# Two sink operations, smaller projection groups in batch 0, and more work that GpSimd and VectorE share, in a planned attention and mixture kernel

## The chip, the cores and the metric

One core of a Trainium2 chip runs the whole kernel in one launch. The metric is device time in microseconds, from several runs. The profile is of one more execution, taken by the hardware profiler.

## What is computed

The input x of a second attention is the output of a first one.

```python
# first: q, k, v of (4, 8, 768, 64); n_sink = 4, window = 128
scores = q @ k^T / 8
keep = (column < 4) | (0 <= row - column < 128)
x = softmax(where(keep, scores, -1e9)) @ v            # -> (4, 768, 512)
# second: four experts e, each with a causal attention over 768 rows, 64 wide
logits = x @ w_gate                                    # (.., 4); the two largest, softmax of both
y_e = softmax(causal(x wq[e] (x wk[e])^T / 8)) @ (x wv[e]) @ wo[e]
out = sum over the two chosen e of weight_e * y_e
```

Float32 is wanted at nearly full precision. The kernel splits an operand into a high part (float32r) and a low part (the rest) and adds three products: high by high, high by low, low by high.

## The kernel before, in words

**Tiling.** The 768 rows of a batch are six row blocks of 128. The first attention is worked in units of one batch and one pair of heads (16 units, names such as "010": batch 0, pair 1, kind 0), the second in units of one batch and one pair of experts (8 units, "001" to "311", kind 1). In a banded unit row blocks 0 and 1 are one piece (edge_rows), blocks 2 and 3 and blocks 4 and 5 are a pair each (both_rows). A pair goes through: scores on TensorE (line 1398), a copy under a mask (1728) and a subtraction with a row minimum (1736) on VectorE, the exponential with its sum on ScalarE (1740), the sum of the parts (1440, 1442) and its inverse (1445), the normalisation by the inverse on GpSimd (1758), transposes on TensorE (1457) which ScalarE or VectorE copy out of PSUM (1254, 1256), a triangular mask on GpSimd (1514), and value products on TensorE (1424, 1428). For the part of a row's band that two blocks share, the kernel uses differences of neighbouring value blocks, dv, made by two GpSimd subtractions per unit (1645).

**Sinks.** A pair's tile p is 128 x 4 x 132: 128 band columns and 4 sink columns for each of four (row block, head). The sinks' weights go into a small tile, psk: two copies of the high part and one of the low part. The function keep makes them with three GpSimd operations (1749, 1753, 1754) from the weights before normalisation and the inverse, and the normalisation then takes the 512 band columns alone (1758). Sink values are multiplied with a selection into the tile vs, once a unit (spread, 1636).

**Weights.** The weights wv, wq, wk, wo are loaded, ScalarE makes the high parts (1189) and GpSimd the low parts (1193), 16 pieces of up to 260 columns.

**Second attention.** For a unit, q and k are projected with the matmuls of line 1831, in two groups of columns for all batches: row blocks 0 to 3 (512 columns) and 4 and 5 (256). A group waits for x of its row blocks from all four head pairs. ScalarE writes the high part (1313), VectorE the low part (1316). Values and gate logits come from line 1858, the output from line 1905.

**Order.** Nothing is issued in the order of the text. Each operation is a step with a priority, a cost for each engine that may run it, and the steps it waits for. Plan.emit simulates the engines and writes out one fixed order for each queue. It takes an engine's next step by readiness, and on TensorE by priority with a price for changing the kind of matmul (STAY, BULK) and one for waiting (HURRY). Table NUDGE adds a number to priorities, by name of step; table ONLY pins a step to one engine; ISSUE, MOVE_TIME and LANDING price transfers. Where TensorE would wait over 220 ns in the first 130 us of the plan, emit puts filler matmuls on the zero tile "nought" (1061, 1064). Transfers are issued by SP and ScalarE alone.

Of the kernel before, what the change touches and what calls it, by code (L numbers as in the profile page):

```python
# [10 lines left out]
F32 = mybir.dt.float32  # L11
# [23 lines left out]
for other in ("ROWS", "FULL", "cols", "rows"):  # L35
# [5 lines left out]
ISSUE, MOVE_TIME, LANDING = 1.4, 1.25, 400  # L41
# [23 lines left out]
    "differences_POOL": 77.0, "000 differences_POOL": -73.3, "000 differences_POOL 0": -19.3, "both_PE": 0.8,  # L65
# [760 lines left out]
    "311 fn_DVEACT 21": ACT, "311 store_SPACT 5": SP,  # L826
}

HURRY = 86.86
STAY = 50.53  # L830
BULK = -58.78
FILL_COST, FILL_KEEP, FILL_END = 220.0, 0.0, 130000.0
# [181 lines left out]
def kernel(  # L1014
# [14 lines left out]
    nc = tc.nc  # L1029
# [683 lines left out]
    def both_rows(prio, acc, i, pair, value, diff, vs, made_vs):  # L1713
# [43 lines left out]
        def norm():  # L1757
            nc.gpsimd.tensor_mul(p.t[:, :, :128], p.t[:, :, :128], f()[:, :, None].to_broadcast([128, 4, 128]))  # L1758
# [255 lines left out]
```

## Time and profile before

| what | value |
|---|---|
| time, median of 3 runs | 369.12 us (368.68 to 370.0) |
| the profiled execution, device time | 368.14 us |
| its span, first to last instruction | 366.2 us |
| TensorE matmul busy | 357.6 us, 98% |
| VectorE, ScalarE, GpSimd busy | 288.4, 262.3, 206.3 us |
| granted TensorE clock | 1.000 |

Matmuls overlap in the pipeline, so their busy time includes waiting that is hidden in it, and filler counts as busy. Where a row gives "x32 | 33.0, 1041", these are the count, the time in us in which at least one of them ran, and the mean ns of one; what follows a second bar is the engine's idle time before them.

### The profile page before, as it was taken

Reading aid. Unit: us, or ns where it says so; the run is one execution under the profiler, and the core shown is the slowest. Engines: PE = TensorE matmul, PEld = TensorE weight load, DVE = VectorE, ACT = ScalarE, POOL = GpSimd, SP = SyncE. Lnnn points to the kernel's source line nnn. Section 1 sums busy time; section 2 is a strip of 40 time slices with the busy share of each in tenths; the row PEclk is TensorE's granted clock in tenths of the full one; section 3 lists DMA queues with packets and bytes.
Section 4 is the critical chain, followed back from the end, with each engine's and each line's share of the span. In section 5 each row is a group of like instructions: output and inputs, shape, how many; then the busy total and the mean of one; then the engine's idle time right before and its main releaser. Section 6 shows DMA issues by size and latency. Waiting matters only on the chain.

```text
span 366.2 us, 13040 instructions
## 1 busy us (share of the span) xinstructions
PE 357.6 (98%) x4708; PEld 311.1 (85%) x4708; DVE 288.4 (79%) x1271; ACT 262.3 (72%) x928; POOL 206.3 (56%) x490
## 2 busy tenths in 40 slices
PE   8998999999999999999999999999999999999996
PEld 7767789988889889888888888988889889988884
DVE  4798979779989996369999988659799967476831
ACT  2778997459987996149888968536989957056951
POOL 5289999858558718326856973143658720160700
PEclk9999999999999999999999999999999999999999
DMA  9983988961281218322897898018920463049512
GB/s 178 177 199 70 184 148 165 170 114 46 47 152 24 48 25 156 95 89 69 243 252 116 199 248 165 2 57 318 238 39 3 135 220 80 2 174 294 140 59 115
DMA packets 134832, 48.10 MB, mean 131 GB/s; under 512 B 121776, under 2 KB 129456, under 8 KB 134768
## 3 DMA queue, kind: packets, MB, share of 16 engines
q1 hardware_dynamic: 108000, 38.75, 45.9%
q10 hardware_dynamic: 26768, 8.52, 9.7%
q8 instruction: 37, 0.61, 0.7%
q14 instruction: 27, 0.22, 0.2%
HBM read 30.88 MB, written 16.12 MB: 128 GB/s over the span
## 4 chain that ended last, share of the span: by engine, by line
PE 87%; DVE 6%; ACT 3%; DMA 2%; issue 1%; SPq 0%; ACTq 0%; DVEq 0%
PE b L1424 21%; PE b L1831 19%; PE b L1385 10%; PE b L1858 10%; PE b L1905 9%; PE b L1457 8%; PE b L1398 5%; PE b L1380 3%; PE b L1428 1%; DVE b L1728 1%; ACT p L1740 1%; DVE p L1736 1%; DVE p L1674 1%; DMA kn<-in_k_dram 1%; DMA qn<-in_q_dram 1%
## 5 line engine op out<-in xcount | busy, mean ns | idle before, releaser
L1610 ACT ACTIVATE p<-p,st 128x256 f32<-128x256 f32 (+5 forms) x96 | 63.5, 665 | 10.1 <-DVE st L1602 9.7
L1740 ACT ACTIVATE p<-p,st 128x132 f32<-128x132 f32 x128 | 51.0, 405 | 5.5 <-DVE st L1736 4.9
L1602 DVE CUSTOM_DVE_ANT_0 p<-b,cmask 128x384 f32<-128x384 f32 (+3 forms) x96 | 45.4, 502 | 2.0 <-ACT p L1263 1.4
L1385 PE MATMUL b<-ks,qs 64*128 64x384 f32 (+3 forms) x384 | 43.6, 341 | 0.0
L1254 ACT ACTIVATE pt<-b 128x256 f32<-128x256 f32 (+3 forms) x100 | 38.4, 416 | 3.2 <-PE b L1457 3.1
L1424 PE MATMUL b<-pt,vn 128*64 128x128 f32 x448 | 39.6, 281 | 0.3
L1457 PE MATMUL b<-ident,p 64*128 64x64 f32 x820 | 38.5, 227 | 0.3 <-POOL p L1758 0.3
L1440 POOL TENSOR_TENSOR st<-st 128x2 f32<-128x2 f32 (+1 forms) x50 | 9.8, 197 | 50.7 <-ACT p L1610 30.9
L1858 PE MATMUL b<-wvh,x 128*128 128x260 f32 x192 | 38.0, 284 | 0.0
L1457 PEld LDWEIGHTS b<-ident,p 64*128 64x128 f32 x820 | 32.4, 138 | 6.1 <-issue 2.2
L1256 DVE COPY pt<-b 128x256 f32<-128x256 f32 (+3 forms) x74 | 33.3, 464 | 4.8 <-PE b L1457 2.7
L1385 PEld LDWEIGHTS b<-ks,qs 64*128 64x128 f32 x384 | 31.1, 187 | 2.9 <-issue 0.7
L1905 PE MATMUL b<-woh,y 128*128 128x512 f32 x96 | 33.2, 400 | 0.0
L1758 POOL TENSOR_TENSOR p<-p,st 128x512 f32<-128x512 f32 x32 | 33.0, 1041 | 0.0
L1679 ACT ACTIVATE p<-p,st 128x128 f32<-128x128 f32 (+1 forms) x64 | 28.9, 454 | 5.5 <-DVE st L1674 5.3
L1831 PE MATMUL b<-x,wqh 128*128 128x512 f32 (+1 forms) x128 | 32.8, 341 | 0.0
L1831 PE MATMUL b<-x,wkh 128*128 128x256 f32 (+1 forms) x128 | 32.6, 341 | 0.0
L1736 DVE CUSTOM_DVE_ANT_0 p<-b,pair_mask 128x132 f32<-128x132 f32 x128 | 32.4, 285 | 0.0
L1858 PEld LDWEIGHTS b<-wvh,x 128*128 128x128 f32 x192 | 30.8, 188 | 0.9 <-DVE st L1445 0.2
L1424 PEld LDWEIGHTS b<-pt,vn 128*64 128x64 f32 x448 | 25.1, 136 | 4.7 <-issue 1.7
L1514 POOL TENSOR_SCALAR_AFFINE_SELECT pt<-pt 128x512 f32<-128x512 f32 x32 | 20.3, 635 | 13.4 <-ACT pt L1254 8.9
L1398 PE MATMUL b<-kx,qn 64*64 64x128 f32 (+2 forms) x768 | 26.1, 277 | 1.5 <-POOL kx L1328 1.5
(133 smaller groups left out, 1001.8 us busy)
## 6 DMA issues: line engine op xcount, KB each, us to landing
qn<-in_q_dram SPq DMA_DIRECT2D x46, 96.0 KB, 2.6
vn<-in_v_dram SPq DMA_DIRECT2D x22, 192.0 KB, 3.5
out_dram<-o ACTq DMA_DIRECT2D x15, 256.0 KB, 2.3
there<-u SPq DMA_DIRECT2D x5, 768.0 KB, 3.5
u<-there SPq DMA_DIRECT2D x20, 192.0 KB, 4.0
kn<-in_k_dram SPq DMA_DIRECT2D x38, 96.0 KB, 2.7
there<-u SPq DMA_DIRECT2D x5, 640.0 KB, 2.9
u<-there SPq DMA_DIRECT2D x20, 160.0 KB, 4.5
```

The source lines that it names most:

```text
L1254: nc.scalar.activation(dst(), src(), AF.Copy)
L1385: nc.tensor.matmul(o, self.qs.t[hs, a, qs], keys(hs, b), start=n == 0, stop=n == 2)
L1398: nc.tensor.matmul(o, self.q_of()[hs, q0 + 64 * h:q0 + 64 * h + 64], ks, start=True, stop=True)
L1424: nc.tensor.matmul(o[e * 64:e * 64 + 64], lhs, rhs, start=e not in self.begun, stop=last and self.done == len(self.steps))
L1457: nc.tensor.transpose(t[g].t[:, n, :], x[gs], ident[gs, gs])
L1602: nc.vector.tensor_tensor_reduce(out=one(e)[:, cs], in0=s2[e].t[:, :(c1 - c0) * 128], in1=mask(c0, c1), scale=times, scalar=st.t[:, 3, es] ...
L1610: nc.scalar.activation(x, x, AF.Exp, bias=st.t[:, 0, es], scale=-1.0, accum_out=st.t[:, 1, es])
L1736: nc.vector.tensor_tensor_reduce(out=p.t[:, n, :], in0=s2[e].t[:, 248 * r:248 * r + SW], in1=pair_mask, scale=-scale, scalar=BIG, op0=OP.a ...
L1740: nc.scalar.activation(p.t[:, n, :], p.t[:, n, :], AF.Exp, bias=st.t[:, 0, n:n + 1], scale=-1.0, accum_out=st.t[:, 1, n:n + 1])
L1831: nc.tensor.matmul(t.t, w[a][:, c, es], X[b, c].t[:, x, cs], start=c == 0 and m == 0, stop=c == NCH - 1 and m == 2)
L1858: nc.tensor.matmul(t.t[:, :VW], X[b, c].t[:, a, qs], W["wv"][w][:, c, :], start=c == 0 and n == 0, stop=c == NCH - 1 and n == 2)
L1905: nc.tensor.matmul(t.t, Y[b, c].t[:, a, qs], W["wo"][w][:, c, :], start=c == 0 and n == 0, stop=c == EP - 1 and n == 2)
```

## The change

Six edits in the kernel's text:

- Sinks. The normalisation takes all 528 columns of p and may run on GpSimd (one operation) or on ScalarE (four). After it a GpSimd copy writes the two high parts of the sinks, and a GpSimd subtraction the low part. The three operations of keep are gone.
- Projections of batch 0. Its column groups become row blocks 0 and 1, 2 and 3, 4 and 5. Batches 1 to 3 keep theirs.
- Low parts of the weights, the low part of the sinks' values, the spreads and the differences may run on VectorE as well as on GpSimd (by_either).
- The tables. NUDGE has some 3,050 entries before and after; of 2,822 names found in both, ten keep their number. ONLY grows from 402 to 442 pins. Among the new ones low parts 1, 10 and 12 are pinned to VectorE and eight to GpSimd, the spreads of units 020 and 100 to VectorE and nine to GpSimd, the differences of 110, 130, 210, 200, 220, 300 and 310 to VectorE and six to GpSimd (010, 020 and 030 among them). Of the pairs' normalisations 000 norm 3, 020 norm 2, 110 norm 2, 120 norm 3 and 330 norm 2 are pinned to ScalarE, nine to GpSimd. What isn't pinned the planner chooses.
- Planner's weights: HURRY 86.86 to 58.27, STAY 50.53 to 53.9, BULK -58.78 to -24.95.
- Transfer prices: ISSUE 1.4 to 1.3, MOVE_TIME 1.25 to 1.15, LANDING 400 to 250.

```diff
+    def by_either(prio, cost, fn, *rest, **more):
+        def go():
+            fn(nc.vector if s.eng == DVE else nc.gpsimd)
+        go.__qualname__ = fn.__qualname__
+        s = plan.step(prio, cost, go, *rest, **more)
+        return s
...
-                    prio + 3, {POOL: 700},
+                    prio + 3, {POOL: 700, DVE: 520},
...
-        lo = plan.step(SINK_VALUES + 1, {POOL: 2430}, lambda: nc.gpsimd.tensor_sub(
+        lo = by_either(SINK_VALUES + 1, {POOL: 2430, DVE: 1600}, lambda engine: engine.tensor_sub(
...
-            made_vs = plan.step(prio_of(max(first, 2)), {POOL: pool_cost(256)}, spread, SINKS[1], [vs], fifo="vs")
+            made_vs = by_either(prio_of(max(first, 2)), {POOL: pool_cost(256), DVE: 420}, spread, SINKS[1], [vs], fifo="vs")
...
-            differ = plan.step(..., {POOL: 2 * (260 + 1.7 * 64 * (end - d0))}, differences, ...)
+            differ = by_either(..., {POOL: 2 * (260 + 1.7 * 64 * (end - d0)), DVE: 1000}, differences, ...)
...
+        def norm():
+            if nm.eng == ACT:
+                for n in range(4):
+                    nc.scalar.activation(p.t[:, n, :], p.t[:, n, :], AF.Copy, scale=st.t[:, 2, n:n + 1])
+            else:
+                nc.gpsimd.tensor_mul(p.t, p.t, f()[:, :, None].to_broadcast([128, 4, SW]))
+        nm = plan.step(prio - LEAD_N, {POOL: pool_cost(4 * SW), ACT: 4 * (187 + 0.833 * SW)}, norm, [r], (), [p, st])
+
         def keep():
-            nc.gpsimd.tensor_mul(psk.t[:, :32]..., p.t[:, None, :, 128:SW]..., f()...)
-            low = psk.t[:, 32:48].rearrange("p (n s) -> p n s", s=4)
-            nc.gpsimd.tensor_mul(low, p.t[:, :, 128:SW], f()[:, :, None].to_broadcast([128, 4, 4]))
-            nc.gpsimd.tensor_sub(psk.t[:, 32:48], psk.t[:, 32:48], psk.t[:, :16])
-        kept = plan.step(prio - LEAD_N, {POOL: 672}, keep, [r], [psk], [p, st], fifo="psk")
-
-        def norm():
-            nc.gpsimd.tensor_mul(p.t[:, :, :128], p.t[:, :, :128], f()[:, :, None].to_broadcast([128, 4, 128]))
-        nm = plan.step(prio - LEAD_N, {POOL: pool_cost(512)}, norm, [r, kept], (), [p, st])
+            sinks = p.t[:, :, 128:SW]
+            nc.gpsimd.tensor_copy(psk.t[:, :32]..., sinks[:, None].to_broadcast([128, 2, 4, 4]))
+            nc.gpsimd.tensor_sub(psk.t[:, 32:48]..., sinks, psk.t[:, :16]...)
+        kept = plan.step(prio - LEAD_N, {POOL: 440}, keep, [nm], [psk], [p], fifo="psk")
...
-            second(b, n, cuts, rows, row, ...)
+            second(b, n, cut("0 2 4 6") if b == 0 else cuts, rows, row, ...)
```

## Rows read from the trace of the kernel before

**Rows 1.** The page's busy times: us, share of the span, instructions of each engine.

```profile
PE 357.6 (98%) x4708; PEld 311.1 (85%) x4708; DVE 288.4 (79%) x1271; ACT 262.3 (72%) x928; POOL 206.3 (56%) x490
```

**Rows 2.** Busy time by stretches of 10 us: the stretch and its length, then busy us and instructions of PE, PEld, DVE, ACT and POOL, the granted clock, the DMA share and GB/s.

```profile
10.00:20.00 10.00, 9.85 (x206) 7.94 (x206) 8.44 (x48) 7.39 (x34) 4.09 (x12) 1.00 1.02 180
20.00:30.00 10.00, 9.17 (x176) 6.97 (x170) 9.72 (x55) 8.38 (x37) 8.66 (x22) 1.00 0.80 170
30.00:40.00 10.00, 8.38 (x168) 7.09 (x166) 8.47 (x54) 8.93 (x39) 9.54 (x16) 1.00 0.53 100
40.00:50.00 10.00, 9.79 (x180) 7.80 (x177) 9.76 (x52) 10.00 (x44) 9.76 (x23) 1.00 0.85 170
50.00:60.00 10.00, 9.66 (x138) 8.61 (x138) 7.53 (x30) 7.54 (x29) 9.92 (x19) 1.00 0.80 155
...
80.00:90.00 10.00, 10.00 (x154) 8.73 (x152) 10.00 (x45) 9.79 (x34) 6.78 (x15) 1.00 0.18 42
...
140.00:150.00 10.00, 10.00 (x69) 9.20 (x68) 3.35 (x19) 3.90 (x16) 8.95 (x22) 1.00 0.82 158
...
270.00:280.00 10.00, 10.00 (x190) 8.90 (x191) 10.00 (x53) 10.00 (x44) 8.39 (x20) 1.00 0.01 3
```

**Rows 3.** The same table for the filler of line 1064 alone: PE and PEld busy us, with their instructions.

```profile
10.00:20.00 10.00, 3.89 (x52) 2.73 (x52) 1.00 1.02 180
20.00:30.00 10.00, 3.13 (x42) 2.17 (x44) 1.00 0.80 170
30.00:40.00 10.00, 1.90 (x36) 1.66 (x32) 1.00 0.53 100
40.00:50.00 10.00, 0.88 (x12) 0.64 (x12) 1.00 0.85 170
50.00:60.00 10.00, 0.00 (x0) 0.00 (x0) 1.00 0.80 155
```

**Rows 4.** The chain that ended last, share of the span by engine, from the page.

```profile
PE 87%; DVE 6%; ACT 3%; DMA 2%; issue 1%; SPq 0%; ACTq 0%; DVEq 0%
```

**Rows 5.** Pieces of that chain in order of time: start us, length us, what.

```profile
4.68 4.11 DMA kn<-in_k_dram
...
12.85 0.42 DVE b L1728
...
22.94 1.09 ACT p L1740 x6
...
41.68 0.31 DVE x L1242
...
52.85 1.75 PE b L1424 x28
```

**Rows 6.** GpSimd's groups by line and shape: out<-in, shapes, count, busy us, mean ns of one, idle us before.

```profile
L1758 POOL TENSOR_TENSOR p<-p,st 128x512 f32<-128x512 f32 x32 | 33.0, 1041 | 0.0
L1645 POOL TENSOR_TENSOR dv<-vn 128x256 f32<-128x256 f32 x32 | 22.9, 735 | 0.9 <-DMA vn<-in_v_dram 0.5 <-PE b L1424 0.3
...
L1749 POOL TENSOR_TENSOR psk<-p,st 128x32 fp32r<-128x32 f32 x32 | 7.6, 239 | 7.4 <-ACT p L1740 4.8 <-DVE st L1445 2.6
...
L1754 POOL TENSOR_TENSOR psk<-psk 128x16 f32<-128x16 f32 x32 | 7.1, 222 | 2.5
L1753 POOL TENSOR_TENSOR psk<-p,st 128x16 f32<-128x16 f32 x32 | 6.9, 215 | 0.0
...
L1328 POOL COPY kx<-kx 128x20 f32<-128x20 f32 x16 | 3.2, 199 | 9.9 <-DVE kx L1355 5.0 <-ACT kx L1254 2.3 <-DVE st L1445 1.9
...
L1193 POOL TENSOR_TENSOR wvl<-v,wvh 128x260 fp32r<-128x260 f32 x4 | 2.9, 734 | 0.0
```

**Rows 7.** The same view of VectorE (one row) and ScalarE.

```profile
L1242 DVE SCALAR_TENSOR_TENSOR x<-b,x 128x256 fp32r<-128x256 f32 x48 | 19.5, 412 | 2.1 <-ACT x L1237 1.8
...
L1689 ACT ACTIVATE p<-p,st 128x128 f32<-128x128 f32 x16 | 5.5, 393 | 0.5 <-DVE st L1442 0.2 <-DVE st L1445 0.2
...
L1313 ACT ACTIVATE ks<-b 128x512 fp32r<-128x512 f32 x8 | 4.8, 596 | 3.7 <-PE b L1831 3.6
...
L1313 ACT ACTIVATE ks<-b 128x256 fp32r<-128x256 f32 x8 | 3.0, 379 | 7.2 <-PE b L1831 7.1
```

**Rows 8.** Timeline of TensorE around 80 us: start us, length us, instruction.

```profile
80.13 0.39 PE L1424 MATMUL b<-pt,vn 128*64 128x128 f32 x4
80.34 0.39 PE L1424 MATMUL b<-pt,dv 128*64 128x128 f32 x4
80.66 0.28 PE L1457 MATMUL b<-ident,psk 64*128 64x64 f32 x2
```

**Rows 9.** Two later pieces of the chain: a unit's 48 projection matmuls, and the 72 value and gate matmuls of a batch (260 columns each).

```profile
211.01 8.63 PE b L1831 x48
...
231.64 8.79 PE b L1858 x72
```

**Rows 10.** A VectorE instruction with two operands in SBUF (line 1889): its shortest, median and longest duration in ns, then the timelines of VectorE and of GpSimd around its first occurrence.

```profile
L1889 DVE SCALAR_TENSOR_TENSOR gate<-gate x4: 173/178/694, 77.3 to 321.1; 128x24 f32<-128x24 f32 x4
...
77.27 0.69 DVE L1889 SCALAR_TENSOR_TENSOR gate<-gate 128x24 f32<-128x24 f32 x1 [0.27 <-POOL gate L1885]
...
77.20 0.73 POOL L1193 TENSOR_TENSOR wol<-o,woh 128x252 fp32r<-128x252 f32 x1
```

More of the change, by code (lines that the diff above doesn't have):

```diff
@@ L823 @@
[L823 to L831 removed]
+    " weight_POOLDVE 0": POOL, " weight_POOLDVE 1": DVE, " weight_POOLDVE 3": POOL, " load_SPACT 1": SP,
@@ new lines @@
+    " weight_POOLDVE 5": POOL, " load_SPACT 2": SP, " weight_POOLDVE 6": POOL, " load_SPACT 3": SP,
+    " weight_POOLDVE 8": POOL, " weight_POOLDVE 9": POOL, " load_SPACT 4": SP, " weight_POOLDVE 10": DVE,
+    " load_SPACT 5": SP, " weight_POOLDVE 12": DVE, " load_SPACT 6": SP, " weight_POOLDVE 14": POOL,
+    " weight_POOLDVE 15": POOL, "000 load_SPACT 1": SP, "000 load_SPACT 2": SP, "000 load_SPACT 3": SP,
+    "000 load_SPACT 4": SP, "000 fn_DVEACT 0": ACT, "000 fn_DVEACT 1": ACT, "000 fn_DVEACT 2": ACT, "000 fn_DVEACT 5": DVE,
@@ L832 @@
+    "311 fn_DVEACT 12": ACT, "311 fn_DVEACT 13": ACT, "311 fn_DVEACT 14": ACT, "311 fn_DVEACT 16": DVE,
+    "311 store_SPACT 0": ACT, "311 fn_DVEACT 17": DVE, "311 fn_DVEACT 18": ACT, "311 store_SPACT 2": SP,
+    "311 fn_DVEACT 19": ACT, "311 fn_DVEACT 20": ACT, "311 store_SPACT 4": SP, "311 fn_DVEACT 21": ACT,
+    "311 store_SPACT 5": SP,
+}
+HURRY = 58.27
+STAY = 53.9
+BULK = -24.95
 FILL_COST, FILL_KEEP, FILL_END = 220.0, 0.0, 130000.0
@@ L1190, in weight @@
                               after=[ld], use=[st])
-                W_READY[name].append(plan.step(
-                    prio + 3, {POOL: 700},
-                    lambda a=a, z=z, to=to, st=st: nc.gpsimd.tensor_sub(lo[:, to], st.t[:, a:z].bitcast(F32), hi[:, to].bitcast(F32)),
+                W_READY[name].append(by_either(
+                    prio + 3, {POOL: 700, DVE: 520},
+                    lambda engine, a=a, z=z, to=to, st=st: engine.tensor_sub(lo[:, to], st.t[:, a:z].bitcast(F32), hi[:, to].bitcast(F32)),
                     [h], (), [st]))
@@ L1632, in band_rows, with spread, differences @@
             vs = buf("vs", 4, D)
-            def spread():
+            def spread(engine):
                 vp = SINKS[0][:, number, :]
-                nc.gpsimd.tensor_mul(vs.t[:48], vp[:48, None, :].bitcast(F32).to_broadcast([48, 4, D]), gsel[:, :, None].to_broadcast([48, 4, D]))
-            made_vs = plan.step(prio_of(max(first, 2)), {POOL: pool_cost(256)}, spread, SINKS[1], [vs], fifo="vs")
+                engine.tensor_mul(vs.t[:48], vp[:48, None, :].bitcast(F32).to_broadcast([48, 4, D]), gsel[:, :, None].to_broadcast([48, 4, D]))
+            made_vs = by_either(prio_of(max(first, 2)), {POOL: pool_cost(256), DVE: 420}, spread, SINKS[1], [vs], fifo="vs")
             dv = buf("dv", NB - 2, 2, D)
             d0, v0 = max(first, 2), 0
-            def differences():
+            def differences(engine):
                 for e in range(2):
                     x = value[2][0].t
-                    nc.gpsimd.tensor_sub(dv.t[:, d0 - 2:end - 2, e, :], x[:, d0 - v0:end - v0, e, :], x[:, d0 - 1 - v0:end - 1 - v0, e, :])
-            differ = plan.step(prio_of(d0) - LEAD_E, {POOL: 2 * (260 + 1.7 * 64 * (end - d0))}, differences, value[1](None), [dv], value[2], fifo="dv")
+                    engine.tensor_sub(dv.t[:, d0 - 2:end - 2, e, :], x[:, d0 - v0:end - v0, e, :], x[:, d0 - 1 - v0:end - 1 - v0, e, :])
+            differ = by_either(prio_of(d0) - LEAD_E, {POOL: 2 * (260 + 1.7 * 64 * (end - d0)), DVE: 1000}, differences, value[1](None), [dv], value[2], fifo="dv")
         for i in range(first, end):
@@ L1977 @@
                 values(b, [(0, NB)], lambda i: at_row(b, 0, 1, 20.0)(i) - (VALUES if b else VALUES_0))
-            second(b, n, cuts, rows, row, lambda i: at_row(b, n, 1, 0.0)(i) - (PREP_2 if b else PREP_3))
+            second(b, n, cut("0 2 4 6") if b == 0 else cuts, rows, row, lambda i: at_row(b, n, 1, 0.0)(i) - (PREP_2 if b else PREP_3))
             if n == EP - 1:
```

220 lines of the change are left out of this document (111 added, 109 removed), and 1336 rows, old and new, of the table NUDGE.

## The prediction

> **What bounds the kernel now.** I read the page's busy shares first: TensorE is marked busy 98% of the span [rows 1]. A share of this kind covers idling dressed as work, so the next view was the table by stretches, and it splits the run in two. From 60 us on TensorE stands at 10.00 of 10 while VectorE, ScalarE and GpSimd vary between a third and full [rows 2]. Up to 60 us it is below that, and its busy time is partly filler: the matmuls on the tile "nought" (line 1064), which the planner puts into TensorE's pauses, take 3.89, 3.13, 1.90 and 0.88 us of the four stretches from 10 to 50 us and nothing from 50 to 60 [rows 3]. With the unmarked 2.81 us (40 less 9.85, 9.17, 8.38 and 9.79) TensorE is without work of its own for 9.80 + 2.81 = 12.6 us between 10 and 50 us. That is nearly all the waiting that shows as such; before it, the first q and k have to land, until 8.8 us [rows 5].
>
> Who is waited for there is said by the chain of waits. Over the whole run it gives 87% to TensorE, 6% to VectorE, 3% to ScalarE and none to GpSimd [rows 4]; in order of time its VectorE and ScalarE pieces lie before 52 us, and from 52.85 us the long pieces are TensorE's [rows 5]. So: a start of 52 us which the elementwise engines set (all three are at work 8 to 10 of 10 from 20 us on), then some 310 us which TensorE sets. The clock granted is 1.00 in every stretch shown, the upper level of 2.4 GHz, and has no part in the argument.
>
> **The change part by part.** A measurement of this kernel can tell 0.3%, 1.1 us, from no change.
>
> *Sinks in two operations.* Per pair of row blocks GpSimd now spends 239 + 215 + 222 ns on the sinks (lines 1749, 1753, 1754) and 1041 ns on the normalisation [rows 6], 1717 ns. After: one normalisation over 528 columns, 1041 ns at least and 1041 x 528/512 = 1074 at most; a copy between 199 ns (line 1328, 20 columns) and 239 ns; a subtraction of 222 ns. That is 1462 to 1535 ns, a saving of 0.18 to 0.26 us, 32 times: 5.8 to 8.2 us of GpSimd's 206 [rows 1, 6]. After 60 us it is worth nothing, as TensorE sets the time. In the start it falls 8 times, 1.4 to 2.1 us; GpSimd isn't on the chain, so it pays only as far as other work moves over. Shared by three engines it is 0.5 to 0.7 us; bounds 0 and 0.7, I take 0.3. By itself it can't cost: every pair gets shorter. But the normalisation may now also run on ScalarE, as four instructions of 344 ns (5.5 us over 16) to 393 ns [rows 7], 1.4 to 1.6 us for GpSimd's 1.05. Two pairs of the start are pinned there, 2.8 to 3.1 us of an engine that has 5.30 us open between 10 and 50 us. Queued behind them are the exponentials and half of the evacuations, and for these wait the transposes and value products. That takes back part of the gain and is kept in the range.
>
> *Three groups of two row blocks in batch 0.* The columns are the same; 48 matmuls of 512 and 256 columns become 72 of 256. A unit's 48 take 8.63 us, 72 of 260 columns take 8.79 [rows 9]. So TensorE pays between 0 and 0.16 us a unit, two units, 0 to 0.3 us; I take 0.2. A gain in TensorE's own work is excluded by the equal columns. ScalarE's splitting goes from 596 + 379 ns to three times 379 [rows 7], +0.16 us, four times, 0.6 us; VectorE's low halves have the same shapes, and I count the same. TensorE's full stretch hides both; uncovered they would cost 0.6. The smaller first group needs only row blocks 0 and 1, so projections can begin sooner. From 60 us that gains nothing; between 40 and 60 us 0.88 + 0.21 + 0.34 = 1.4 us are left to fill [rows 2, 3]. Bounds 0 and 1.4, counted in the balance below.
>
> *Low parts, differences, spreads on either engine.* GpSimd pays 734 ns for a low part of a weight and 2 x 735 ns for a unit's differences [rows 6]. The trace has nothing of this form and size on VectorE. The nearest row is its subtraction of 256 columns out of PSUM, 412 ns [rows 7]; GpSimd's own time bounds it from above, from below the 0.31 us of such a piece in the chain [rows 5]. I take 412. A moved low part relieves GpSimd by 0.73 us and loads VectorE by 0.41. Of those pinned, three of eleven low parts, two of eleven spreads and seven of thirteen differences go to VectorE, none of these differences in batch 0; the rest is left to the planner. Seven differences are 7 x 2 x 0.41 = 5.8 us more on VectorE after 60 us, hidden as long as TensorE has work in hand.
>
> A row speaks against this part. Line 1889, a VectorE instruction of 24 columns with both operands in SBUF, takes 173, 178 (the median) and once 694 ns; that once it began at 77.27 us, while GpSimd's subtraction of a weight's low part ran from 77.20 for 0.73 us, and it ended 0.04 us behind it [rows 10]. So it seems that such an instruction stands until GpSimd's is done. The moved ones are all of this form. In the start GpSimd is 9.5 of 10 busy from 30 us [rows 2], so each of the three low parts and two spreads would wait half an instruction, 0.37 us: 1.8 us on VectorE. A quarter of that on the path is 0.5, which I charge; bounds 0 and 1.8.
> The Trainium skill has a rule for this (SBUF — State Buffer, section Who interferes with whom): a VectorE instruction with two SBUF inputs contends with a GpSimd instruction that reads SBUF, and the later of the two waits the other out. The row of 694 ns agrees with it; without rule or row the sum would be 0.5 us lower.
>
> *The new order.* The tables of nudges and pins are replaced, along with the planner's weights and DMA prices, so every queue is re-ordered. No row prices that, so it is bounded. The open time from 10 to 50 us is 3.61 us on VectorE, 5.30 on ScalarE and 7.95 on GpSimd [rows 2], 16.9 together. If a plan with more choice of engine used all of it, the stage would be 16.9/3 = 5.6 us shorter; if none, 0; if the moved work lands on the two engines of the chain, up to 3 us longer (the two ScalarE normalisations). I take half, 2.8 us, because work that was tied to GpSimd can now give way, and the chain's two engines have open time of their own. After 60 us I take 0: TensorE's work stays, and only the number of changes between kinds of matmul can differ. Value products follow one another by 0.21 us, and the step from them to the transposes is 0.32 [rows 8], so a change costs some 0.1 us.
>
> *Transfers.* The planner's DMA prices fall, so it places loads later. The first k takes 4.11 us [rows 5] and is waited for in both kernels; I count 0, and up to 1 us if one of batch 0's loads comes late.
>
> **Sum.** -2.8 (balance of the start) - 0.3 (sinks) + 0.2 (groups) + 0.5 (VectorE behind GpSimd) = -2.4 us. The profiled run took 368.14 us, 366.2 of span and 1.9 around it, so it would be 365.7. The median of the runs is 369.12, 1.0 above the profiled one, so I predict 369.1 - 2.4 = 366.7 us.
>
> **The rivals.**
> *A, VectorE becomes the bound.* Slower. VectorE is at 9.72 to 10.00 of 10 already in several stretches (20 to 30, 40 to 50, 80 to 90, 270 to 280 us [rows 2]), and work moves to it. Place: the banded units of batches 1 to 3, where the value products wait for differences. Price: half of the 5.8 us uncovered is 2.9; the gain of the start is then eaten by the rest, and the time is 372 us. It decides once VectorE has no open time in such a stretch while TensorE's ready work runs out. For it: those tens. Against it: stretches like 140 to 150 us, VectorE at 3.35 [rows 2], can absorb a shift. Chance 0.08.
> *B, VectorE and GpSimd block one another* as in rows 10, all over the run. 7 x 2 differences, 3 low parts and 2 spreads, 19 instructions, wait 0.37 us each, and GpSimd's stand 0.41 behind them in turn: 19 x 0.78 = 15 us of engine time. A third on the path is 5 us, against the gain of 2.9 that is 371.2. Against it: after 60 us both engines have slack. Chance 0.11. It is the rule named above at its full price.
> *C, nothing comes of it.* The chain of the start goes through VectorE and ScalarE; relief of GpSimd doesn't shorten it, and the order elsewhere is as good as before: 369.1, within 1.1. Chance 0.18.
> *D, fewer changes of kind.* The weights that set when TensorE stays with a kind are changed too. By [rows 8] a change costs 0.1 us; with 130 of them after 60 us (an estimate: the timeline around [rows 8] has some 13 in 10 us, and about ten such stretches are mixed) a third fewer is 4.3 us on top of 2.4: 362.4. For it: each is on the path. Against it: their number follows from dependences. Chance 0.11.
> *The forecast*, 363.5 to 368 us: 0.52.
>
> **How the numbers follow.** Faster by over 0.3%: 0.52 + 0.11 = 0.63. Within: 0.18. Slower: 0.08 + 0.11 = 0.19. The range goes from 361.5, below D, to 371.5, which takes in C and B's price and leaves out A and the tails. The forecast's own range is 363.5 to 368.
>
> **What would show it.** Right: filler and unmarked time of TensorE between 10 and 50 us fall from 12.6 to about 10 us, the long TensorE pieces of the chain begin near 50 us instead of 52.85, TensorE takes as long from there as before, and the two sink operations stand at some 0.2 us each. Wrong: filler as before and the gain elsewhere (D: fewer steps of 0.32 us between kinds), VectorE's subtractions well over 0.41 us beside GpSimd work (B), or new pauses of TensorE behind VectorE after 80 us (A).

## The result and the profile after

The kernel after takes 373.05 us (median; 370.57 to 373.79), the kernel before, timed beside it, 368.62: a ratio of 1.0106 [1.0086, 1.0125], slower by 4.4 us by the medians and 3.9 by the ratio. I had predicted 366.7 us and a range of 361.5 to 371.5, so the sign is wrong and the range doesn't hold the time. The profiled run shown here took 373.78 us, 372.1 of them span.

From the page of the kernel after: the busy line, the granted clock over 40 slices, and the shares of the chain that ended last.

```profile
PE 359.3 (97%) x4710; PEld 315.9 (85%) x4710; DVE 293.6 (79%) x1278; ACT 284.3 (76%) x992; POOL 174.4 (47%) x425
...
PEclk9997899999999999999999999999999999999999
...
PE 77%; DVE 5%; POOL 5%; DMA 5%; ACT 3%; SPq 3%; issue 1%; ACTq 0%; POOLq 0%; DVEq 0%
```

GpSimd is relieved by 32 us against [rows 1], as planned. Yet it has come onto the chain, where it had no share [rows 4], and TensorE's share fell from 87% to 77%. The digit 7 in the clock is new.

The stretches that answer to [rows 2], in the same columns:

```profile
10.00:20.00 10.00, 8.91 (x184) 7.33 (x182) 7.03 (x38) 8.01 (x34) 3.72 (x8) 1.00 0.82 162
20.00:30.00 10.00, 9.03 (x196) 7.41 (x188) 8.81 (x52) 9.12 (x38) 7.16 (x15) 1.00 0.98 204
30.00:40.00 10.00, 7.71 (x92) 6.26 (x94) 8.38 (x43) 8.73 (x38) 7.44 (x18) 0.67 0.66 140
40.00:50.00 10.00, 9.70 (x160) 8.10 (x158) 8.71 (x43) 7.72 (x30) 6.25 (x13) 0.99 0.42 87
50.00:60.00 10.00, 8.64 (x153) 7.29 (x150) 9.96 (x45) 9.75 (x42) 9.77 (x18) 1.00 1.00 178
```

And the filler of what is now line 1070, which answers to [rows 3]:

```profile
10.00:20.00 10.00, 3.57 (x56) 2.71 (x50) 1.00 0.82 162
20.00:30.00 10.00, 3.06 (x44) 2.34 (x44) 1.00 0.98 204
30.00:40.00 10.00, 0.00 (x0) 0.00 (x0) 0.67 0.66 140
40.00:50.00 10.00, 0.00 (x0) 0.00 (x0) 0.99 0.42 87
```

Filler and unmarked time of TensorE between 10 and 50 us were to fall from 12.6 to about 10 us. They are 6.63 + 4.65 = 11.3. That looks like half a success, but filler became standing still: from 30 to 40 us there is none, TensorE is marked 7.71, and the granted clock is 0.67 on average. From 50 to 60 us TensorE is unmarked for another 1.36 us, against 0.34 before.

To see where the loss arises I added up, from the records of matmuls, the work of TensorE's own that is done by a given time (each matmul with the interval of its shape in full flow, filler not counted), and took the difference to the kernel before. It is good to some 0.5 us, since the order of the work differs, and it compares one profiled run of each kernel. In us, less than nothing meaning behind:

```
by                   40     60     80    130    150    200    250    320    350
after              -1.9   -2.7   -3.2   -3.5   -4.1   -3.7   -5.0   -5.6   -5.3
e9_store_sp        -0.4   -0.3   -1.1   -1.1   -2.0   -1.4   -1.3   -2.8   -3.5
e10_either          0.0   -0.2   -0.5   -1.3   -1.6   -2.4   -2.7   -2.9   -2.7
e13_late           -0.2   -0.2   -0.2   -1.3   -1.6   -2.4   -2.7   -2.8   -2.6
e12_early           0.0   -0.2   -0.5   -0.6   -0.9   -0.9   -1.0   -0.9   -0.9
```

More than half of the loss is there by 80 us, the rest comes after. The places where the trace shows TensorE standing say for whom it waits; these are its groups in the trace after (line, shape, count, busy, mean, and last the idle time before them with what ended it):

```profile
L1438 PE MATMUL b<-pt,vn 128*64 128x128 f32 x448 | 39.6, 282 | 1.2 <-ACT pt L1268 1.1
...
L1412 PE MATMUL b<-kx,qn 64*64 64x128 f32 (+2 forms) x768 | 28.2, 286 | 1.7 <-POOL kx L1342 1.3 <-ACT p L1693 0.4
...
L1438 PE MATMUL b<-u,v 128*64 128x128 f32 x300 | 18.6, 274 | 1.6 <-DMA u<-there 1.6
...
L1471 PE MATMUL b<-ident,kn 64*128 64x64 f32 x48 | 3.0, 236 | 1.3 <-ACT pt L1268 1.3
```

Four waits, four releasers: ScalarE (ending at 55.16 us), GpSimd (34.11), a transfer (231.13), ScalarE (30.62). VectorE has none of the large ones, and after 60 us the transfer's is the only one over a quarter of a microsecond.

**The wait at 33 us and the clock.** First GpSimd's timeline (start, us, line), then TensorE's, then single microseconds (the columns of [rows 2]):

```profile
31.52 1.07 POOL L1767 TENSOR_TENSOR p<-p,st 128x528 f32<-128x528 f32 x1 [0.33 <-DVE st L1459]
32.66 0.21 POOL L1772 CAST psk<-p 128x32 fp32r<-128x32 f32 x1
32.95 0.22 POOL L1773 TENSOR_TENSOR psk<-p,psk 128x16 f32<-128x16 f32 x1
33.20 0.72 POOL L1207 TENSOR_TENSOR wol<-o,woh 128x252 fp32r<-128x252 f32 x1
33.86 0.20 POOL L1342 COPY kx<-kx 128x20 f32<-128x20 f32 x1
34.02 0.60 POOL L1650 TENSOR_TENSOR vs<-vp,gsel 48x256 fp32r<-48x256 f32 x1
```

```profile
34.11 1.58 PE L1412 MATMUL b<-kx,qn 64*64 64x196 f32 x24 [1.33 <-POOL kx L1342]
```

```profile
32.00:33.00 1.00, 0.78 (x11) 0.56 (x11) 1.00 (x9) 1.00 (x6) 0.85 (x3) 1.00 0.43 105
33.00:34.00 1.00, 0.00 (x0) 0.00 (x0) 0.93 (x6) 1.00 (x6) 0.97 (x3) 0.66 1.07 292
34.00:35.00 1.00, 0.89 (x18) 0.89 (x22) 0.94 (x2) 1.00 (x5) 0.62 (x2) 0.50 1.09 172
...
39.00:40.00 1.00, 1.00 (x14) 0.96 (x12) 0.79 (x4) 0.07 (x1) 1.00 (x2) 0.50 1.03 234
```

TensorE waits for a copy of 20 columns that stands in GpSimd's queue behind a weight's low part of 0.72 us which only the output projections need, much later. The granted clock falls to its lower level at 33.33 us, within this pause, and stays there until 40.16 us, 6.8 us by the clock's records. Pauses of 1.29 and 0.34 us, behind copies of ScalarE and VectorE, went before. The kernel before stood at the same copy even longer, 1.52 us, but behind 54 filler matmuls, and kept the upper level:

```profile
28.79 3.12 PE L1064 MATMUL b<-nought 128*64 128x128 f32 x54
...
34.31 0.90 PE L1398 MATMUL b<-kx,qn 64*64 64x196 f32 x24 [1.52 <-POOL kx L1328]
```

**Transfers on the chain.** Pieces of the chain of waits of the kernel after (start, us, what), from two places:

```profile
42.44 2.85 DMA vn<-in_v_dram
45.31 2.15 DMA v<-in_moe_w_gate_dram
...
341.71 5.24 DMA out_dram<-o
...
347.79 2.52 DMA u<-there
```

SyncE gives the load of the gate weights out at 45.31 us, 6.2 us after it could, when a load of v has landed that ScalarE gave out and with which it shares no buffer. The last read-back of unit 301 (its tile u, loaded again from device memory), under way from 347.79 us, was held in the same way by the landing of an output store. Both are waits of one transfer for an unrelated one of another queue.

### The profile page after: what moved, and what is told of

It is laid out like the page before. It is cut to its first block, busy times and chain, and to the rows that moved or that the text cites. A ratio compares the mean times of both kernels' runs of the same rounds, so it can differ in the third digit from the quotient of the medians.

```text
span 372.1 us, 13098 instructions
## 1 busy us (share of the span) xinstructions
PE 359.3 (97%) x4710; PEld 315.9 (85%) x4710; DVE 293.6 (79%) x1278; ACT 284.3 (76%) x992; POOL 174.4 (47%) x425
## 4 chain that ended last, share of the span: by engine, by line
PE 77%; DVE 5%; POOL 5%; DMA 5%; ACT 3%; SPq 3%; issue 1%; ACTq 0%; POOLq 0%; DVEq 0%
PE b L1438 18%; PE b L1846 16%; PE b L1920 9%; PE b L1873 9%; PE b L1471 8%; PE b L1399 7%; PE b L1412 5%; PE b L1394 2%; DMA u<-there 2%; SPq L1814 1%; DMA out_dram<-o 1%; DVE p L1616 1%; PE b L1931 1%; PE b L1442 1%; POOL p L1767 1%
## 5 line engine op out<-in xcount | busy, mean ns | idle before, releaser
L1624 ACT ACTIVATE p<-p,st 128x512 f32<-128x512 f32 (+5 forms) x96 | 63.5, 665 | 7.7 <-DVE st L1616 7.4
L1268 ACT ACTIVATE pt<-b 128x256 f32<-128x256 f32 (+3 forms) x106 | 41.1, 420 | 6.7 <-PE b L1471 5.6
L1454 POOL TENSOR_TENSOR st<-st 128x4 f32<-128x4 f32 (+1 forms) x56 | 11.5, 206 | 69.8 <-ACT p L1624 32.5
L1471 PE MATMUL b<-ident,p 64*128 64x64 f32 x820 | 39.9, 226 | 0.0
L1873 PE MATMUL b<-wvh,x 128*128 128x260 f32 x192 | 36.5, 284 | 0.0
L1846 PE MATMUL b<-x,wqh 128*128 128x256 f32 (+1 forms) x144 | 33.3, 320 | 0.0
L1270 DVE COPY pt<-b 128x256 f32<-128x256 f32 (+2 forms) x68 | 30.1, 456 | 3.7 <-PE b L1471 3.1
L1528 POOL TENSOR_SCALAR_AFFINE_SELECT pt<-pt 128x512 f32<-128x512 f32 x32 | 20.4, 638 | 24.6 <-ACT pt L1268 15.1
L1693 ACT ACTIVATE p<-p,st 128x256 f32<-128x256 f32 (+1 forms) x64 | 28.6, 449 | 3.8 <-DVE st L1688 3.7
L1412 PE MATMUL b<-kx,qn 64*64 64x128 f32 (+2 forms) x768 | 28.2, 286 | 1.7 <-POOL kx L1342 1.3
L1561 DVE STREAM_TRANSPOSE u<-u 128x640 f32<-128x640 f32 (+2 forms) x30 | 23.7, 824 | 6.4 <-ACT u L1277 3.6
```

The costliest lines, as they stand in the source:

```text
L1268: nc.scalar.activation(dst(), src(), AF.Copy)
L1412: nc.tensor.matmul(o, self.q_of()[hs, q0 + 64 * h:q0 + 64 * h + 64], ks, start=True, stop=True)
L1471: nc.tensor.transpose(t[g].t[:, n, :], x[gs], ident[gs, gs])
L1624: nc.scalar.activation(x, x, AF.Exp, bias=st.t[:, 0, es], scale=-1.0, accum_out=st.t[:, 1, es])
L1846: nc.tensor.matmul(t.t, w[a][:, c, es], X[b, c].t[:, x, cs], start=c == 0 and m == 0, stop=c == NCH - 1 and m == 2)
L1873: nc.tensor.matmul(t.t[:, :VW], X[b, c].t[:, a, qs], W["wv"][w][:, c, :], start=c == 0 and n == 0, stop=c == NCH - 1 and n == 2)
```

## The experiments

Sixteen kernels, each timed beside the kernel before, whose median in these jobs was 368.53 to 368.68. Medians in us, number of runs, ratio to before:

```
after            373.05  8  1.0106 [1.0086, 1.0125]
e1_fill          372.15  6  1.0092 [1.0068, 1.0117]
e2_vn_sp         371.79  6  1.0077 [1.0052, 1.0103]
e3_fill_vn_sp    371.80  6  1.0093 [1.0066, 1.0119]
e4_low_after_kx  371.73  5  1.0084 [1.0064, 1.0104]
e5_store         371.56  6  1.0087 [1.0066, 1.0108]
e6_store_load    371.69  5  1.0087 [1.0074, 1.0099]
e7_pool_back     374.55  5  1.0170 [1.0154, 1.0185]
e8_sinks_only    369.21 12  1.0014 [1.0001, 1.0026]
e9_store_sp      371.81  4  1.0089 [1.0075, 1.0103]
e10_either       371.66  4  1.0086 [1.0072, 1.0100]
e11_sinks_fill   370.01  5  1.0042 [1.0028, 1.0055]
e12_early        369.14 11  1.0012 [1.0002, 1.0023]
e13_late         370.27  5  1.0047 [1.0034, 1.0059]
e14_norms        373.62  4  1.0135 [1.0122, 1.0149]
e15_late_back    372.64  5  1.0101 [1.0086, 1.0115]
e16_early_back   372.28  6  1.0104 [1.0084, 1.0124]
```

Most edits act on the finished plan: PAUSES puts filler ahead of a named step, RUN_ON gives a step to another engine at its place in the order, MOVES puts a step behind another. Otherwise the order is untouched.

### Mending the kernel after: e1 to e6, e9

```diff
# e1_fill
+PAUSES = {'030 tr_PE 1': 5, '030 quarters_PE 0': 6}
# e2_vn_sp
+RUN_ON = {"030 load_SPACT 2": SP}
# e3_fill_vn_sp: both of them
# e4_low_after_kx
+MOVES = [(' weight_POOLDVE 13', '030 go_POOL 0', 1)]
```

> The changed kernel, every queue in its own order, with 22 filler matmuls more on the zero tile: five pairs ahead of the transposes of unit 030 near 29 us and six pairs ahead of its scores, where TensorE stood from 32.8 to 34.1 us of the profiled run and the clock granted went to 0.50 from 33.3 to 40.2 us. Theory clock: those 6.8 us at half clock cost about 3 us, as the work done by 40 us lags 1.9 us behind the kernel before and the rest of the gap opens directly behind. It expects a granted clock of 1.00 throughout and 369.5 to 371 us, 2 to 3.5 less than the changed kernel's 373.05. Rival order: TensorE only waited for the elementwise engines there, so it will do its work faster and wait longer behind them; clock 1.00, but 372.5 to 373.5 us.

> The changed kernel in its own order; only the load of v for unit 030, which ScalarE's queue issued at 42.4 us, is issued by SP's queue, behind the load of the gate weights. Theory false wait: SP stood 6.2 us, until 45.3 us, in front of the load of the gate weights for that load of v, which has nothing to do with it; so the value weights' low parts began on GpSimd at 48.05 us, and the chain then ran on GpSimd until 63 us. It expects the load of the gate weights near 39 us, the first low part of wv before 46 us, and 370.5 to 372 us, 1 to 2.5 less than 373.05. Rival: GpSimd is full from 50 to 70 us anyway (9.8 and 8.7 of 10) and the low parts had been early enough; then 372.5 to 373.5 us.

> Both of the edits before together. If clock and false wait each cost what their theories say and lie one behind the other, 367.5 to 370 us, at or below the kernel before (368.6). If the two losses hide one another, no better than the better one of the two alone, 369.5 to 371. If neither is a cause, 372.5 to 373.5.

> The changed kernel in its own order but for one pair on GpSimd: the low part of a piece of wo (0.72 us at 33.20) comes after the small copy of sink keys of unit 030 (line 1342) instead of before it. TensorE's scores waited 1.33 us for that copy. Theory GpSimd on the chain: the scores begin 0.5 to 0.7 us sooner, and if that makes the pause short enough for the clock to stay, 370 to 371.5 us with a clock of 1.00; if the clock falls all the same, about 372.4. Rival: the copy waited for its keys and not for the low part, then nothing moves, 372.5 to 373.5 us.

With the filler the clock is 1.0 in all six runs of e1, where it is 0.99 in all eight of the kernel after, and in the profiled run TensorE is 1.6 us behind at 80 us where it was 3.2. By the medians each of the three edits e1, e2 and e4 is worth 0.9 to 1.3 us, by the ratios 0.5 to 1.1; their intervals overlap that of the kernel after, so no single one is clear of the noise. e1 doesn't reach what its theory asked for (371 or less), and its filler isn't free:

```profile
30.87 1.31 PE L1078 MATMUL b<-nought 128*64 128x128 f32 x20 [1.29 <-ACT pt L1276]
...
33.72 1.53 PE L1078 MATMUL b<-nought 128*64 128x128 f32 x24
35.18 0.90 PE L1420 MATMUL b<-kx,qn 64*64 64x196 f32 x24
```

The first block stands behind the pause of 1.29 us and not in it, and the second runs on after GpSimd's copy has ended, at 34.32 us. From the end of the 1.29 us pause to the scores it takes 4.31 us, against 3.49 in the kernel after: 0.8 us later, by the experiment's own doing. So e1's gain is what the clock gives back less this delay, and e3, e5, e6, e9, e15 and e16 carry the same filler.

e2 sends the load of the gate weights at 39.18 us as expected, but the first low part of wv begins at 47.21 us and not before 46. Under e4 the scores wait 0.54 us instead of 1.33, and the clock still falls (0.990), at 31.36 us, before that pause begins and behind those of 1.29 and 0.34 us alone. So the wait for the copy isn't what brought the clock down there, and no run separates what the clock costs from what the pauses cost. The edits don't add up: e3 with two of them stands at 371.80, where e2 alone stood. In e3 TensorE's work is level with before's from 80 to 140 us and then falls behind again, to 3.3 us at 350 us. What the start gives back is lost later.

```diff
# e5_store: e3 and
+MOVES = [('211 store_SPACT 2', '301 back_SP 2', 1)]
# e6_store_load: e5 and
+MOVES = [..., ('330 load_SPACT 1', '111 back_SP 2', 1)]
# e9_store_sp: e6 and
+RUN_ON = {..., "211 store_SPACT 2": SP}
```

> The kernel of e3 (filler and load of v by SP), and one more false wait taken out at the end: the output store of row block 2 of batch 2, issued by ScalarE, stands in ScalarE's queue behind the last read-back of the tiles u of unit 301 and not ahead of it. In e3's profile SP's issue of that read-back waited for this store's landing until 343.3 us, and TensorE's next value products began at 347.83 behind the read-back. Theory false waits: TensorE gets its operands about 2 us sooner in the last stage; 369.5 to 371 us, against 371.8 of e3, and the chain shows no landing of an output store before 350 us. Rival: other work fills the wait and the queue of products is as long; 371.5 to 372.5.

> The kernel of e5, and the load of k for unit 330 (four transfers) comes behind the two last read-backs of u of unit 111 in SP's queue, not ahead of them. In the changed kernel's profile that load took SP from 219.3 to 225.1 us, the read-back landed at 231.0 and TensorE lost 1.1 us there; e1's and e3's profiles don't show the loss, so it comes in some runs only. Theory: the spread of the runs (370.6 to 373.8 us of the changed kernel, 2 us in e1 to e3) comes in part from this place; spread under 1.5 us and a median 0 to 1 us below e5. Rival: the load comes late for unit 330 itself; as e5 or up to 1 us above.

> The kernel of e6_store_load with the output store of unit 211 that held up the last read-back issued by SyncE, behind the read-backs, in place of ScalarE. In e6 the chain shows 5.04 us of that store's landing, then 2.97 us of the read-back, then TensorE at 348.54 after 0.93 us without work. Theory that the read-back waits for the landing of a store that it has nothing to do with: the landing leaves the chain, the read-back is issued some us earlier, and the time falls by the 0.9 us that TensorE stood and what trails it, to 370.5 to 371. Rival, that the end is set by the engines and the wait is a shadow of it: 371.7 again. If neither load, store nor clock is left and the time stays above 370, what remains (1.5 us or more) is the order of the steps itself.

e5 missed its aim: the read-back still waits for that store. The runs of e6 spread over 0.7 us and its median is as before. That the load is what spreads them isn't shown: e4 without the edit spreads over 1.0 us, e16 with it over 2.8. e9 takes the store off the chain at 341 us and is no faster. The theory that the transfers at the end cost a microsecond falls. What stands in e9 in place of them (groups of TensorE with their idle time):

```profile
L1456 PE MATMUL b<-pt,vn 128*64 128x128 f32 x448 | 39.2, 281 | 1.2 <-ACT pt L1286 1.1
...
L1456 PE MATMUL b<-u,v 128*64 128x128 f32 x300 | 18.7, 274 | 0.7 <-issue 0.7
...
L1460 PE MATMUL b<-sk,vs 64*128 64x128 f32 x64 | 12.6, 282 | 0.5 <-ACT o L1286 0.5
```

Three stops, ending at 52.7, 344.9 and 252.3 us, of 1.1, 0.7 and 0.5 us. With the clock and the known transfers mended, 3.2 us remain. They aren't the sum of these stops. By the table e9 is 0.3 us behind at 60 us, after the first stop and after its own filler, and 3.5 at 350; of the 3.2 us lost between, TensorE is unmarked for 1.3. The rest lies in time in which it is marked busy.

### One part alone in the order before: e8, e11, e10, e12, e13

```diff
# e8_sinks_only
         def keep():
-            nc.gpsimd.tensor_mul(psk.t[:, :32]...
-            ...
+            pass
+
+        def keep_after():
+            sinks = p.t[:, :, 128:SW]
+            nc.gpsimd.tensor_copy(psk.t[:, :32]..., sinks[:, None].to_broadcast([128, 2, 4, 4]))
+            nc.gpsimd.tensor_sub(psk.t[:, 32:48]..., sinks, psk.t[:, :16]...)
...
-            nc.gpsimd.tensor_mul(p.t[:, :, :128], p.t[:, :, :128], ...)
+            nc.gpsimd.tensor_mul(p.t, p.t, f()[:, :, None].to_broadcast([128, 4, SW]))
+            keep_after()
# e11_sinks_fill: e8 and
+PAUSES = {'000 tr_PE 5': 3, '020 tr_PE 0': 4}
```

> The kernel before, in its own order and with its own tables; only the sinks are made in two operations: one GpSimd normalisation over 528 columns, then a copy and a subtraction, 32 times (1085 + 216 + 224 = 1525 ns in the changed kernel, against 1717). My prediction's step: 0 to 0.7 us less than before, 0.3 taken; 367.9 to 368.6. If the new way of making the sinks were itself at fault for the slowdown (the transposes now wait for three operations in a row behind the inverse, not for the normalisation alone), over 369.5.

> The kernel of e8_sinks_only (the order before, sinks in two operations) with 14 more filler matmuls in the two pauses of TensorE between 22.4 and 24.5 us, which were 0.33 and 0.44 us long. Theory that the half us that e8 stood above the kernel before is the drop of the clock that sets in at 24.6 us in most of its runs: the granted clock is 1.0 in all runs here and the time is 368.4 to 368.9, no different from before. Rival, that the sinks in two operations cost by themselves (the normalisation with 528 columns delays the transposes behind it): 369.2 again with a clock of 1.0.

The sinks in two operations gain nothing: +0.5 us. The four runs of e8 with a clock of 1.0 take 368.5 to 368.9, so up to 0.3 from before; those with less, up to 370.3. In its profiled run the clock drops at 24.6 us for 3.4 us, behind TensorE's short pauses at 22.4 and 24.0, and TensorE is 1 us behind from there to the end. The kernel before has such runs too, fewer of them. So at a like clock the two operations cost 0.2 us or nothing. e11 was to separate the two, and didn't. Its first filler went into a pause, its second landed behind one:

```profile
24.54 1.09 PE L1072 MATMUL b<-nought 128*64 128x128 f32 x16 [0.47 <-ACT kx L1262]
```

The filler writes a PSUM bank that came free only with what the pause waited for, so 1.09 us of filler stands on the path. The time is 370.01, against 369.21 of e8 and 368.5 to 368.9 of its runs at full clock: 0.8 to 1.5 us more. So at 24 us there is little slack or none.

```diff
# e10_either
+RUN_ON = [" weight_POOL 12", " weight_POOL 10", " weight_POOL 1", "020 spread_POOL 0", ...]   # 15 steps
-                nc.gpsimd.tensor_mul(vs.t[:48], ...
+                on().tensor_mul(vs.t[:48], ...
...
# e12_early: the first 8 of the 15, e13_late: the other 7
```

> The kernel before with its order untouched, and the same 15 steps that the change moves to VectorE (4 low parts of weights, 4 spreads, 7 pairs of differences) run by VectorE at the place that they had in GpSimd's turn. In the order after, moving these 15 back to GpSimd cost 1.5 to 1.9 us. Theory that the choice of engine is good in itself and the new order is what costs: 367.5 to 368.8 here, since GpSimd is on no piece of the chain before, so that at most a few tenths can be had. Rival A (VectorE becomes what TensorE waits for): 370 or more. Rival B (VectorE and GpSimd hold one another up): each of the 15 about 0.28 us longer than alone, and 369.5 to 370.5.

> The order before with only the first eight of the 15 steps on VectorE (4 low parts of weights, 3 spreads, 1 pair of differences, all before 75 us; 9 instructions of about 0.41 us, 3.7 us of VectorE). Theory that the start is set by the chain through VectorE and ScalarE, so that what VectorE is given there comes out at the end in good part: 370.0 to 370.8, and TensorE's work about 1 us behind from 70 us on. Rival, that the steps after 75 us are what costs: 368.6 to 369.2.

> The order before with only the other seven on VectorE (1 spread, 6 pairs of differences, between 83 and 214 us; 13 instructions, 5.3 us of VectorE). The forecast took these as hidden behind TensorE's work: 368.4 to 368.9. Theory that VectorE's turn is so tight that they are not: 370 to 371, with the loss at 130 to 140 and 190 to 200 us, where e10 lost 0.6 and 0.8 us.

This is the finding of the study. The 15 steps on VectorE cost 3.05 us in the order before, where each keeps the place that it had in GpSimd's turn; another place in VectorE's own turn wasn't tried. I had expected at most a few tenths, since in the order after they gain. And the larger part is where I had looked for nothing: the seven late ones cost 1.7 us, the eight early ones 0.6, where e12's theory had asked for 1.5 or more. Pieces of e13's chain of waits (start, us, what), the row of TensorE's timeline at its end, and the stretch from 190 to 200 us in before and in e13:

```profile
173.35 0.76 DVE u L1557
174.11 0.64 DVE dv L1655 x2
174.75 0.07 DVE st L1455
174.82 0.74 DVE u L1557
...
177.41 1.09 ACT p L1620 x4
...
187.57 1.94 ACT p L1750 x10
189.51 0.49 ACT ks L1323
...
190.02 0.70 DVE ks L1326
```

```profile
190.77 0.70 PE L1390 MATMUL b<-kx,qn 64*128 64x128 f32 x5 [0.60 <-DVE ks L1326]
```

```profile
190.00:200.00 10.00, 10.00 (x198) 9.09 (x190) 9.89 (x51) 8.95 (x37) 4.71 (x13) 1.00 0.76 142
190.00:200.00 10.00, 9.40 (x178) 8.22 (x178) 9.96 (x48) 7.93 (x32) 4.88 (x13) 1.00 0.91 187
```

The pair of differences, "dv", stands between two transposes that VectorE makes of u. The chain leads from its 0.64 us through VectorE, ScalarE's exponentials and a piece of GpSimd, 16 us later, to TensorE, which is marked 10.00 of 10 all the way from 170 to 190 us. That it works off its stock of ready work meanwhile, and stands when that is gone, is my reading. The stop of 0.60 us is all that shows: from 60 to 360 us TensorE is unmarked for 0.61 us in e13 and for nothing in before, yet e13 falls 2.4 us further behind in that time. Some 1.8 us of the loss lie in time marked busy, and no row says where. From 170 to 180 and from 180 to 190 us VectorE is busy 9.7 and 9.6 of 10, ScalarE 9.7 and 8.2. The loss stays: 2.4 us behind at 200 us and 2.6 at 350.

### The other way, in the order after: e7, e14, e15, e16

```diff
# e7_pool_back: all 15 steps; e15_late_back, e16_early_back: the 7 or the 8, on top of e9
+RUN_ON = {" weight_POOLDVE 12": POOL, ..., "310 differences_POOLDVE 0": POOL}
# e14_norms
+RUN_ON = {"000 norm_POOLACT 3": POOL, "010 norm_POOLACT 2": POOL, "020 norm_POOLACT 2": POOL, "110 norm_POOLACT 2": POOL}
```

> The changed kernel in its own order; the 15 steps that the plan gave to VectorE (four low parts of weights, four spreads, the differences of seven units) run on GpSimd again, at the same place of the order. Theory lock: VectorE's instructions with two SBUF operands stood behind GpSimd's (low parts of 652 to 844 ns against 451) and lengthened some of GpSimd's; if that is a main cause of the slowdown, 371 to 372 us. Rival relief: the moved work is worth its place on VectorE, as GpSimd is on the chain from 48 to 63 us and gets 0.73 us more for each of eight steps there; 374 to 376 us. Neither: 372.5 to 373.5.

> The order after with the four normalisations of banded pairs that ScalarE has before 75 us (4 instructions of about 0.4 us each) run by GpSimd at the same place (1.085 us each). Theory that ScalarE's added work is a cause of the loss in the start: below 373 by 0.5 to 1.5 us, 371.5 to 372.5. Rival, that in this order GpSimd is on the chain between 31 and 63 us and can't take more: 374 to 376. As for e7, a cost both ways says that the order and the choice of engine can't be changed one without the other.

> The kernel of e9_store_sp (the order after, with more filler, the two loads and the store mended; 371.8) with the seven steps that VectorE has after 75 us run by GpSimd at the same place. Theory that VectorE's turn between 100 and 270 us is what makes the kernel after slow, as in e13: 370 to 371. Rival, that the order was made for this choice and the loss lies in the order itself: 371.8 or up to 1 us more.

> The same kernel with the eight steps that VectorE has before 75 us run by GpSimd in place of the late ones. In the order after GpSimd is on the chain from 31 to 63 us, so theory and rival agree on no gain here: 372 to 374. A time below 371.5 would say that VectorE is what the start waits for in this order too.

No step pays when it is given back: e7 is 1.5 us slower than the kernel after, clear of its interval; e14 is 0.6 above it, and e15 and e16 are 0.8 and 0.5 above e9, within their intervals. In e14 TensorE's wait for GpSimd's small copy grows from 1.33 to 2.75 us, so GpSimd has no room at that place. So it isn't the engine of these steps that makes the kernel after slow. The 15 steps cost 3.05 us on VectorE in the order before and 1.5 on GpSimd in the order after: the choice of engine can't be judged without the order. What this leaves open is below.

## Why the prediction was wrong

**What bounds the kernel.** I read off the chain that VectorE and ScalarE set the start and that GpSimd is absent from it [rows 4]. The first half is borne out in part only: e12 gives VectorE 3.7 us more before 75 us and loses 0.6. The second I wrote down, and counted a gain from relieving GpSimd all the same. The other half of the picture, that TensorE alone sets the time from 52.85 us on, is what e13 refutes: 10.00 of 10 says that TensorE had something to do, not that the others could lag without harm.

**The new order, -2.8 us.** This is the step that failed, and with it the sign. I added up the open time of three engines [rows 2], called it 5.6 us, took half as gained in the start, and 0 after 60 us. In place of 2.8 us ahead, TensorE's own work is 2.7 us behind at 60 us, and in place of 0 it loses another 2.6 from there to 350; the chain's long TensorE pieces begin at 63.5 us and not near 50. Open time isn't there to be filled: I had no row that says what ended it. The order after loses at 33 us by an order within GpSimd's queue, loses its filler and with that the upper level of the clock, stands behind ScalarE for 1.3 us at 30 and 1.1 at 54 us, and loses at transfers. e1, e2 and e4 put 0.9 to 1.3 us each on three of these by the medians, not additive and none clear of the noise; the stops behind ScalarE weren't tried. My upper bound for this term was 3 us of loss, for work that lands on the two engines of the chain. Measured against before, the whole change costs 4.4.

**VectorE, +0.5 and "hidden after 60 us".** The sizes were right: differences 411 ns, against 0.41 assumed. The lock with GpSimd is there too. This is the group of VectorE's differences and spreads, and the row of the low part of the output weights, which began at 34.06 us, 0.04 behind GpSimd's spread of the timeline above:

```profile
L1659 DVE TENSOR_TENSOR dv<-vn 128x256 f32<-128x256 f32 x14 | 5.2, 411 | 0.0
...
L1650 DVE TENSOR_TENSOR vs<-vp,gsel 48x256 fp32r<-48x256 f32 x4 | 2.5, 618 | 0.0
```

```profile
34.06 0.84 DVE L1207 TENSOR_TENSOR wol<-o,woh 128x260 fp32r<-128x260 f32 x1
```

It takes 0.84 us and ends 0.28 after GpSimd's. Five of the 22 moved instructions took 0.65 to 0.87 us, some 1.9 us longer in all, what I had worked out from [rows 10] (1.8). The Trainium skill (SBUF — State Buffer, section Who interferes with whom) says that a VectorE instruction with two SBUF inputs contends with a GpSimd instruction that reads SBUF; the trace agrees, with all five ending 0.27 to 0.29 us after a GpSimd instruction that ran beside them. Wrong was the price on the path. I charged 0.5 for the start and nothing later; in the order before, e12 and e13 measure 0.6 and 1.7, and together 3.05.

**Sinks, -0.3 us.** The operations came out as worked out, 1085 + 216 + 224 = 1525 ns per pair against 1462 to 1535:

```profile
L1767 POOL TENSOR_TENSOR p<-p,st 128x528 f32<-128x528 f32 x22 | 23.8, 1085 | 8.3 <-DVE st L1459 8.2
...
L1773 POOL TENSOR_TENSOR psk<-p,psk 128x16 f32<-128x16 f32 x32 | 7.2, 224 | 2.6
L1772 POOL CAST psk<-p 128x32 fp32r<-128x32 f32 x32 | 6.9, 216 | 2.7 <-ACT p L1765 2.1
```

```profile
L1765 ACT ACTIVATE p<-p,st 128x132 f32<-128x132 f32 x40 | 12.9, 400 | 0.0
```

The saving is on an engine that nobody waited for, and the 0.3 us didn't come: e8 is 0.5 us above before, [0.0, 1.0], and 0.2 at a like clock. Ten pairs are normalised by ScalarE, 4 x 400 ns each, which I had priced at 1.4 to 1.6; but I had counted two of them in the start, and there are four before 75 us.

**Groups, +0.2.** Not tried alone; no run prices it. **Transfers, 0.** Wrong in place: not batch 0's first loads but transfers that wait for unrelated ones. Mending one gained 1.3 us by the medians (e2), not clear of the noise; mending the next ones gained nothing (e5, e6, e9).

**The rivals.** A came near with its time, 372, by luck. Its mechanism, work that moves to an engine without room, exists in the order before (e13: 1.7 us for six of the seven pairs of differences and a spread, against A's 2.9). In the kernel after its sign is missing, a pause of TensorE behind VectorE after 80 us, and e15, which takes these steps off VectorE, isn't faster. I had given it 0.08, because a stretch with VectorE at 3.35 could absorb a shift; in e13 none did. B's lock is real and small. C (nothing comes of it) rested on the sentence that relief of GpSimd doesn't shorten the chain, which is right. D is out: it wanted a third fewer changes of kind, and counted by line or by shape of the matmuls they are as many as before within some 5 per cent.

**Still open.** About 3 us of the 4.4 remain with the clock and the transfers that I could name mended (e9), and e15 and e16 don't find them in the engine of a step. They are lost after 60 us, where e9 is only 0.3 us behind, its own filler included. The stops in e9's trace don't make up the rest: after 60 us TensorE is unmarked for 1.3 us, where before has none, and the first stop lies ahead of the loss. One rival was left untried. ScalarE is busy 22 us more than before (284.3 against 262.3), 17.5 of them after 60 us, more than VectorE gained in all (5.2); the pairs' normalisations are 12.9 of it, and e14 took back four of the ten. Whether the late ones hold TensorE up isn't shown. No version beat the kernel before; the nearest, e12 and e8, are 0.5 us above it.

## What to carry to other kernels

Relief of an engine that nothing waits for on the chain is no gain by itself, and the work goes to one that may be waited for. Give the moved work a price on the receiving engine also where the matmul engine is marked full: here 5.3 us of it cost 1.7, and 3.7 us cost 0.6. Open time of an engine isn't a reserve that a new order can spend; look at what ended it. And look in a changed plan for pauses of TensorE that lost their filler: the clock fell in one here, and held in all six runs of e1 with filler back. Filler has to be able to start before the pause ends, or it stands behind it, as in e1 and e11.

## What the hardware showed that I had not expected

The granted clock fell to its lower level 0.55 us into a pause that began at 32.78 us and followed pauses of 1.29 and 0.34 us, and stayed there for 6.8 us; in e4 it fell behind the two alone. In e8's profiled run two pauses of 0.33 and 0.44 us went before a drop of 3.4 us, while pauses of 0.31 and 0.48 us at the same place in before's went without one. The kernel before stood for 1.52 us behind 3.12 us of filler and kept the upper level. VectorE, when it had to wait for GpSimd's instruction, ended 0.27 to 0.29 us after it in all five cases. And a load given out by SyncE waited 6.2 us for a load of ScalarE's queue that it had nothing to do with.
